# The end of a transformer block rearranged into strands on their own PSUM banks, with 1/sqrt on GpSimd

## The chip, the cores and the metric

The kernel runs on one core of a Trainium2 chip. The metric is the device time of one execution in microseconds (us); less is better. Times of several executions are given as a median with their range. The profile is of one further execution.

## What is computed

One block with adaptive layer norm: attention with 32 heads of 16 columns over 2048 tokens of width 512, then a gated feed-forward network (FFN) of width 1792. Inputs and output are bf16. `B_x` is not used.

```python
def _layernorm(x, axis=-1, eps=1e-05):
    return (x - mean(x)) / sqrt(var(x) + eps)
def _A_ref(x, wqkv, wo):              # H = 32, Dh = 16
    q, k, v = heads(x @ wqkv)
    p = softmax(q @ k.T * Dh ** -0.5)
    return merge(p @ v) @ wo
def _B_ref(x, w_gate, w_up, w_down):
    return (gelu(x @ w_gate) * (x @ w_up)) @ w_down
sa, ca, ga, sb, cb, gb = split(silu(c) @ w_mod, 6)
h = _layernorm(x) * (1 + ca) + sa
x = x + ga * _A_ref(h, A_wqkv, A_wo)
h = _layernorm(x) * (1 + cb) + sb
x = x + gb * _B_ref(h, B_w_gate, B_w_up, B_w_down)
```

## The kernel before

The names of engines: PE does matmuls, ACT (ScalarE) activations, DVE (VectorE) and POOL (GpSimd) elementwise work, SP issues DMAs.

**Recorder and planner.** The whole program is written by a planner in Python that runs when the kernel is built. `rec` notes each instruction with what it reads and writes and works out the semaphore waits; `model` and `cost` keep an estimate of the time at which each engine is free. Each engine then executes its own list in order, and waits only where a semaphore says so. Side work is kept as generators (`side_wo`, `side_ffn`, `near_end` and others) and as tasks, lists of steps for one engine after another, which `step` places when the estimate says that their inputs are there. Matmuls of zero value to the result, here called fillers, are put in when the estimate (`short`, `FILL`) shows PE less busy than wanted.

**Attention.** The 2048 query tokens are cut into seven sets, `SETS`, of 512, 512, 256, 256, 256, 128 and 128. Within a set the heads go in eight groups of four (`qd`), spread over the four 32-row strips of PE. Score matmuls write to `ps_sc`, six banks of PSUM used as two halves of three; one ACT instruction does the exponential of up to three banks (1536 columns) into `E`, and now and then one bank is given to DVE instead, which does an exponential in seven steps (`exp_vec`). A gate on `credit` and the backlog decides when. The PV matmuls add into `ps_pv`; V has a column of ones, so that one output row of 17 is the softmax's denominator. `pv_round` copies the finished group to `osb`, takes the denominator out through DRAM (`scr_den`, `den`, reciprocal into `rden`, `scr_rec`) and spreads it over partitions into `rb` with four DMAs; then `onorm` = `osb` x `rb`. The last groups (`qd` 6 and 7) of the last two sets do without DRAM: a matmul with the selector `self32` spreads the denominator in PSUM, and DVE takes the reciprocal of it (`near_end`).

**Behind each set.** `side_wo` multiplies `onorm` with `wo` in bank `ps_mi` and adds to x in `xs`; then come statistics (`ln_stat`: bn_stats, bn_aggr), 1/sqrt(var + eps) in eight small DVE instructions (`ln_rstd_step`: a bit-trick guess and two Newton steps), the normalise (`ln_norm`), transposes, modulation, and the FFN (`side_ffn`), also through `ps_mi`, with gelu made of tanh. All this runs beside the attention of the next sets, in the one bank `ps_mi`.

**The end** (`tail`). Call the last two token tiles A (set 5) and B (set 6). `side_ffn` does the first two chunks (`EARLY`) of A's FFN in `ps_mi`. When A's part is done and all attention with all PV matmuls has been written, `tail` loads ACT's gelu table and interleaves two generators: `tail_end` for B (denominators of group 7 in a bank of `ps_sc`, `wo` into `ps_sc` bank 4 over an identity matmul of x, statistics, normalise, transposes, modulation, then `tail_ffn` on six banks) and `tail_ffn` for the rest of A on banks 0 to 3, with A's down projection in `ps_pv` and B's in `ps_mi`. The denominator of B's group 6 is a side work item behind A's part, in `ps_mi`. An ACT copy puts B's attention output from PSUM to `xs`, and the statistics of B follow that copy; modulation of B is shared, half on ACT and half on DVE.

Of the kernel before, what the change touches and what calls it, by code (L numbers as in the profile page):

```python
# [5 lines left out]
ACT = mybir.ActivationFunctionType  # L6
# [41 lines left out]
EARLY = 2  # L48
BACK = 10
# [28 lines left out]
class _Recorder:  # L78
# [165 lines left out]
    def model(self, op, t, cost):  # L244
# [38 lines left out]
    def cost(self, eng, out, ins, kind):  # L283
# [8 lines left out]
        if eng == "pool":  # L292
            return n * 3.0 + 100
# [117 lines left out]
class _Kernel(_Recorder):  # L411
# [12 lines left out]
    def alloc(self):  # L424
# [41 lines left out]
        self.nwx = sb("nwx", [P, NT], FP32)  # L466
# [4 lines left out]
        self.nb = sb("nb", [P, NT], FP32)  # L471
# [16 lines left out]
    def prologue(self):  # L488
# [24 lines left out]
        self.affine_select(self.ident[:, :], [[-1, P]], ALU.not_equal, 1.0, 0, 1)  # L513
        self.memset(pool, self.rm4[:, :], 1.0)
# [4 lines left out]
        self.memset(pool, self.vaug[:, :, :].rearrange("p t (h c) -> p t h c", c=VW)[:, :, :, DH:VW], 1.0)  # L519
# [13 lines left out]
        self.ln_rstd(0, 4)  # L533
        self.mod_cols(self.scp[:, 1, 0:8], 0)
# [35 lines left out]
    RSTD = 8  # L570

    def ln_rstd_step(self, a, b, i):

        x, y, t = self.nwx[:, a:b], self.rstd[:, a:b], self.nwt[:, a:b]
        if i == 0:
            self.ts("dve", x, self.mv[:, a:b, 1], EPS, -0.5, ALU.add, ALU.mult)
        elif i == 1:
            self.ts("dve", y.bitcast(I32), x.bitcast(I32), -0.5, 1597463007.0 - 2.0 ** 30 - 2.0 ** 22, ALU.mult, ALU.add)
        elif i % 3 == 2:
            self.tt("dve", t, y, y, ALU.mult)  # L580
        elif i % 3 == 0:
            self.tt("dve", t, t, x, ALU.mult)
        else:
            self.stt(y, t, 1.5, y, ALU.add, ALU.mult)

    def ln_rstd(self, a, b):
        for i in range(self.RSTD):
            self.ln_rstd_step(a, b, i)
# [3 lines left out]

    def ln_nb(self, a, b):
        self.stt(self.nb[:, a:b], self.mv[:, a:b, 0], -1.0, self.rstd[:, a:b], ALU.mult, ALU.mult)

    def ln_norm_pool(self, t, dst):
        self.ts("pool", dst, self.xs[:, t, :], self.rstd[:, t:t + 1], self.nb[:, t:t + 1], ALU.mult, ALU.add)
# [124 lines left out]
    def side_first(self):  # L722
# [4 lines left out]
        def norms(t0):  # L727
            g = t0 // 4
            self.task([lambda i=i: self.ln_rstd_step(t0, t0 + 4, i) for i in range(self.RSTD)]
                      + [lambda t=t: self.ln_norm(t0 + t, self.tb1[:, g % 2, t, :]) for t in range(4)], ("ln", g),  # L730
                      self.after([("st", t) for t in range(max(8, t0), t0 + 4)]))
# [256 lines left out]
    def background(self, t):  # L988
        while self.free["dve"] <= t + 150 and self.step("dve", max(self.free["dve"], t) + 40):
            pass  # L990

    def force(self):
        if not self.step("dve", None):
            assert self.step("act", None)

    def plan(self, ends, nsplit):
# [25 lines left out]
        w.append((lambda: self.near_end(k + 1, 6, self.mi[:, 0:P]), s0, s0))  # L1022
# [48 lines left out]
    def stream(self):  # L1071
# [37 lines left out]
        filler = self.ident[:, :], self.km[0][:, 0, 0:512]  # L1109
# [26 lines left out]
        while rp < len(rounds):  # L1136
# [19 lines left out]
            if tq is not None and tq <= t + 30:  # L1156
# [78 lines left out]
        self.tail(len(SETS) - 2, len(SETS) - 1)  # L1235
# [57 lines left out]
    def pv_round(self, rnd, acc):  # L1293
# [5 lines left out]
        if r != NKT // kpb - 1:  # L1299
            return  # L1300
# [4 lines left out]
        if sets[0] >= len(SETS) - 2 and len(sets) == 1 and qd >= 6:  # L1305
# [34 lines left out]
    def tail(self, ka, kb):  # L1340

        self.require([("part", ka)])
        self.act(self.tcol[:, 0:1], self.tcol[:, 0:1], ACT.Gelu_apprx_tanh)
        gens = [self.tail_end(kb), self.tail_ffn(ka, self.pv[:, :], range(0, 4), 0)]
        nxt = [None] * len(gens)
        while True:
            t = self.pe_now()
            while self.step("act", max(self.free["act"], t) + 40) or self.step("dve", max(self.free["dve"], t) + 40):
                pass
# [23 lines left out]
            if best is None:  # L1373
                if all(g is None for g in gens) and not self.tasks and not self.work:
                    break
                continue
            f, nxt[best[1]] = nxt[best[1]], None
            f()

    def tail_end(self, k):  # L1380
# [3 lines left out]
        bank = self.scp[:, 4, :]  # L1384
        for x in self.near_end(k, 7, self.scp[:, 5, 0:W]):
            if x is not END:
                yield x and x[1]
# [5 lines left out]
        self.task([lambda: self.ln_stat(tile, bank)] + self.ln2_steps(k, bank), ("ln2", k))  # L1393
        self.task([("act", lambda: self.act(self.xs[:, tile, :], bank, ACT.Copy))], ("x1", k))
        yield from self.until(("ln2", k))
        for h in range(2):
            pb = self.scp[:, 4 + h, :]
# [7 lines left out]
    def tail_ffn(self, k, down, banks, e0):  # L1405
# [3 lines left out]
        nb = [0]  # L1409

        def up(ci, w):
            if nb[0] == 2 and k == len(SETS) - 1:
                yield from self.until(("p", k - 1, len(chunks) - 1))
            bk = self.scp[:, banks[nb[0] % len(banks)], :]
# [5 lines left out]
        first = EARLY if k < len(SETS) - 1 else 0  # L1420
# [3 lines left out]
        for ci in range(first, len(chunks) + 1):  # L1424
            if ci < len(chunks):
# [4 lines left out]
                          ("g", k, ci))  # L1430
# [54 lines left out]
```

## Time and profile before

| | us |
|---|---|
| median of 3 runs | 908.53 |
| range of these | 906.87 to 908.95 |
| the profiled execution | 911.24 |
| its span in the trace | 909.4 |
| busy in the span: ACT | 877.2 (96%) |
| DVE | 833.9 (92%) |
| PE | 826.3 (91%) |
| POOL | 3.6 |

All times in the trace are in us from the start of the span, and lengths of single instructions in us or, where it says mean, in ns. PE's busy time counts overlapping matmuls once; PEld is its weight load. The span is the part that the trace covers; the rest of an execution's time lies around it. A group's row gives line, engine, operation, output and input names and shapes, the count, then busy time and mean length of one in ns, then the idle time ahead of them and what ended it. PEclk is the granted clock of PE as a share of full speed.

### The profile page before, as it was taken

How to read it: one execution, taken by the hardware profiler on the slowest of the kernel's cores; microseconds unless marked ns; L12 is line 12 of the kernel's file. 1: busy time of each engine (PE TensorE's matmuls, PEld its weight loads, DVE VectorE, ACT ScalarE, POOL GpSimd, SP SyncE). 2: the span in 40 equal slices, each digit the busy share in tenths (PEclk: the TensorE clock that was granted, in tenths of full speed). 3: DMA queues.
4: the chain of work that ended last, by engine and by line, in shares of the span. 5: the costliest groups of instructions: out<-in, count | busy, mean ns of one | idle time of the engine just before them, and what ended most of it. 6: DMA issues, size and time to landing. Idle time of an engine off the chain costs nothing.

```text
span 909.4 us, 20886 instructions
## 1 busy us (share of the span) xinstructions
PE 826.3 (91%) x8708; PEld 292.0 (32%) x8708; DVE 833.9 (92%) x2114; ACT 877.2 (96%) x754; POOL 3.6 (0%) x11
## 2 busy tenths in 40 slices
PE   8899998988899899998999999999999988989988
PEld 3333322222222222222233222333443334334455
DVE  7779999999998999999998999998999889989874
ACT  5999999999999999999999999999999999999992
POOL 1000000000000000000000000000000000000000
PEclk9999999999999999999999999999999999999999
DMA  9001320000100000000000000000000000000000
GB/s 300 2 25 41 118 86 13 13 15 13 54 13 14 1 13 14 13 14 25 20 14 14 14 9 13 16 25 20 15 8 20 19 9 14 20 15 14 18 11 13
DMA packets 35337, 25.19 MB, mean 28 GB/s; under 512 B 19053, under 2 KB 31082, under 8 KB 35242
## 3 DMA queue, kind: packets, MB, share of 16 engines
q1 hardware_dynamic: 32858, 22.28, 8.7%
q10 hardware_dynamic: 2384, 1.57, 0.6%
q8 instruction: 68, 1.11, 0.5%
q14 instruction: 27, 0.22, 0.1%
HBM read 21.23 MB, written 2.61 MB: 26 GB/s over the span
## 4 chain that ended last, share of the span: by engine, by line
ACT 83%; PE 6%; DVE 5%; DMA 4%; SPq 1%; issue 0%; DVEq 0%
ACT E L319 81%; PE ps_sc L306 3%; ACT wreg L319 2%; PE ps_mi L306 2%; DMA rb<-scr_rec 1%; DMA scr_rec<-rden 1%; SPq L369 1%; DMA mreg<-in_w_mod_dram 1%; PE ps_pv L306 1%; DMA den<-scr_den 0%; DVE qT L323 0%; DVE qT L336 0%; DVE dx L331 0%; DVE wreg L323 0%; DVE wreg L340 0%
## 5 line engine op out<-in xcount | busy, mean ns | idle before, releaser
L319 ACT ACTIVATE E<-ps_sc 128x1536 bf16<-128x1536 f32 (+2 forms) x698 | 849.9, 1440 | 10.6 <-PE ps_sc L306 10.1
L306 PE MATMUL ps_pv<-E,vaug 128*17 128x256 bf16 (+2 forms) x2912 | 182.4, 300 | 1.8 <-DVE vaug L340 0.8
L306 PE MATMUL ps_sc<-qT,kme 32*128 32x256 bf16 (+2 forms) x1600 | 169.0, 304 | 12.9 <-ACT E L319 8.0
L306 PE MATMUL ps_sc<-qT,kmo 32*128 32x256 bf16 (+2 forms) x1664 | 169.1, 298 | 11.4 <-ACT E L319 7.8
L306 PE MATMUL ps_sc<-kme,ident 128*128 128x512 bf16 x334 | 106.7, 384 | 35.5 <-ACT E L319 32.0
L331 DVE TENSOR_SCALAR dt<-ps_sc 128x512 int32<-128x512 f32 x189 | 129.6, 687 | 5.7 <-PE ps_sc L306 3.0
L306 PE MATMUL ps_mi<-wreg,mreg 128*128 128x256 bf16 (+2 forms) x624 | 118.4, 308 | 6.8 <-DVE wreg L340 3.9
L306 PEld LDWEIGHTS ps_sc<-qT,kme 32*128 32x128 bf16 x1600 | 48.7, 92 | 127.0 <-ACT E L319 70.4
L306 PEld LDWEIGHTS ps_sc<-qT,kmo 32*128 32x128 bf16 x1664 | 49.8, 92 | 121.4 <-ACT E L319 70.8
L306 PEld LDWEIGHTS ps_pv<-E,vaug 128*17 128x17 bf16 x2912 | 53.7, 88 | 100.5 <-issue 88.5
L331 DVE TENSOR_SCALAR dx<-dt 128x512 f16<-128x512 uint16 x189 | 78.2, 420 | 0.1
L323 DVE TENSOR_TENSOR qT<-qT,dx 128x512 f16<-128x512 f16 x188 | 77.0, 419 | 0.7
L306 PEld LDWEIGHTS ps_mi<-wreg,mreg 128*128 128x128 bf16 x624 | 49.6, 97 | 55.0 <-issue 21.4
L336 DVE SCALAR_TENSOR_TENSOR qT<-dt,qT 128x512 int16<-128x512 int32 x94 | 64.4, 686 | 0.4
L306 PE MATMUL ps_mi<-dreg,hreg 128*128 128x512 bf16 x210 | 62.7, 384 | 0.8 <-DVE wreg L336 0.3
L323 DVE TENSOR_TENSOR ed<-ed,dx 128x512 f16<-128x512 f16 x128 | 53.1, 419 | 0.5
L306 PEld LDWEIGHTS ps_sc<-kme,ident 128*128 128x128 bf16 x334 | 22.6, 97 | 90.4 <-ACT E L319 87.7
L336 DVE SCALAR_TENSOR_TENSOR ed<-dt,ed 128x512 int16<-128x512 int32 x64 | 43.9, 686 | 0.2
L340 DVE CAST wreg<-ps_mi 128x512 bf16<-128x512 f32 x51 | 35.1, 688 | 8.1 <-PE ps_mi L306 7.5
L306 PE MATMUL ps_mi<-hreg,wreg 128*128 128x512 bf16 x120 | 39.4, 386 | 0.7 <-DVE qT L331 0.2
L323 DVE TENSOR_TENSOR wreg<-wreg 128x512 bf16<-128x512 bf16 (+1 forms) x74 | 38.6, 521 | 0.2
L306 PE MATMUL ps_mi<-wo,onorm 128*128 128x512 bf16 x120 | 35.3, 384 | 1.4 <-DVE xw L323 1.3
(135 smaller groups left out, 770.7 us busy)
## 6 DMA issues: line engine op xcount, KB each, us to landing
rb<-scr_rec SPq DMA_DIRECT2D x64, 64.0 KB, 2.0
rb<-scr_rec SPq DMA_DIRECT2D x116, 32.0 KB, 1.8
mreg<-in_w_mod_dram SPq DMA_DIRECT2D x1, 2048.0 KB, 14.3
out_dram<-xs SPq DMA_DIRECT2D x16, 128.0 KB, 1.7
mreg<-in_B_w_gate_dram SPq DMA_DIRECT2D x4, 448.0 KB, 5.2
mreg<-in_B_w_up_dram SPq DMA_DIRECT2D x4, 448.0 KB, 5.0
dreg<-in_B_w_down_dram SPq DMA_DIRECT2D x3, 512.0 KB, 4.9
wreg<-in_A_wqkv_dram SPq DMA_DIRECT2D x3, 384.0 KB, 10.6
```

The lines of the kernel that those rows point to most:

```text
L306: return self.rec("pe", lambda e: e.matmul(out, lhsT, rhs, start=start, stop=stop, tile_position=tp), [lhsT, rhs], [out], cost=(n, int(rhs ...
L319: return self.rec("act", lambda e: e.activation(out, in_, func, scale=scale, **kw), rd, wr, cost=self.cost("act", out, [in_], "act"))
L323: return self.rec(eng, lambda e: e.tensor_tensor(out, a, b, op), [a, b], [out], cost=self.cost(eng, out, [a, b], "tt"))
L331: return self.rec(eng, lambda e: e.tensor_scalar(out, a, s1, s2, **kw), rd, [out], cost=self.cost(eng, out, [a], "ts" if len(rd) == 1 else ...
L336: return self.rec("dve", lambda e: e.scalar_tensor_tensor(out, a, s, b, op0=op0, op1=op1), rd, [out], cost=self.cost("dve", out, [a, b], " ...
L340: return self.rec(eng, lambda e: e.tensor_copy(out, in_), [in_], [out], cost=self.cost(eng, out, [in_], "ts"))
L369: return e.dma_start(out, in_)
```

## The change

The diff does the following.

- **1/sqrt.** `ln_rstd_step` and its eight DVE steps go. `ln_rstd` is two POOL instructions: add eps, then raise to the power -0.5 held in `half`. The tasks that used the steps now hold one POOL step, and `background`, `force` and `tail` also serve tasks of POOL. The cost estimates for POOL are changed. The memset of the ones in `vaug` moves behind the first such pair on POOL.
- **Statistics ahead of the copy.** In `tail_end` the statistics of B come first, and the ACT copy of the bank, as well as the 1/sqrt and the normalise, wait for them. All four modulations of B are on ACT.
- **Strands and banks.** The main loop ends when the last score matmul has been written (`pos < nseq`), no longer with the last PV; the remaining PV rounds become a generator `rest` of `tail`. The denominators of B's groups 6 and 7 are generators of their own (`tail_den`), each with its own bank. The six banks of `ps_sc` are split in two lists of three: `f` for B (denominators, `wo`, transposes, then its FFN), `l` for the rest of A.
- **Order.** B's steps are put at the head of the task list; A's `tail_ffn` waits for its part by a key in place of `tail` waiting at once. The gelu table is loaded once A's second tanh is written. `tail` may write fillers.
- **The late gate.** An exponential goes to DVE only while `credit` is under 1600, in place of 2600, from the end of the fifth set on.

```diff
+NEAR = 6
...
-            op.t1 = t + cost + (107 if eng == "act" else 92)
+            op.t1 = t + cost + {"act": 107, "dve": 92, "pool": 120}[eng]
...
-            return n * 3.0 + 100
+            return n * (30.0 if n <= 4 else 3.0) + 200
...
+        self.memset(pool, self.half[:, :], -0.5)
...
     def ln_rstd(self, a, b):
-        for i in range(self.RSTD):
-            self.ln_rstd_step(a, b, i)
+        r = self.rstd[:, a:b]
+        self.ts("pool", r, self.mv[:, a:b, 1], EPS, None, ALU.add)
+        self.tt("pool", r, r, self.half[:, 0:b - a], ALU.pow)
...
-        return ([lambda i=i: self.ln_rstd_step(a, b, i) for i in range(self.RSTD)]
+        return ([("pool", lambda: self.ln_rstd(a, b))]
...
-        w.append((lambda: self.near_end(k + 1, 6, self.mi[:, 0:P]), s0, s0))
...
-        while rp < len(rounds):
+        while pos < nseq:
...
-                        and len(mem) == CH and slack > -100 and self.credit < 2600):
+                        and len(mem) == CH and slack > -100 and self.credit < (2600 if pos < ends[-3] else 1600)):
...
-        self.tail(len(SETS) - 2, len(SETS) - 1)
+
+        def rest():
+            for k in range(rp, len(rounds)):
+                while True:
+                    for a in list(active):
+                        if a[0] in self.have:
+                            self.slot[a[1]] = a[2]
+                            active.remove(a)
+                    if pv_ready(k) is not None:
+                        break
+                    yield None
+                yield lambda k=k: self.pv_mms(rounds[k], acc_of(rounds[k]))
+                self.pv_done(rounds[k], acc_of(rounds[k]))
+        self.tail(len(SETS) - 2, len(SETS) - 1, c % 2, rest())
...
-    def tail(self, ka, kb):
-
-        self.require([("part", ka)])
-        self.act(self.tcol[:, 0:1], self.tcol[:, 0:1], ACT.Gelu_apprx_tanh)
-        gens = [self.tail_end(kb), self.tail_ffn(ka, self.pv[:, :], range(0, 4), 0)]
+    def tail(self, ka, kb, half, rest):
+        f = [self.scp[:, CH * half + i, :] for i in range(CH)]
+        l = [self.scp[:, CH * (1 - half) + i, :] for i in range(CH)]
+        gens = [rest] + [self.tail_den(kb, qd, f[qd - 5]) for qd in range(NEAR, 8)]
+        gens += [self.tail_end(kb, f, l), self.tail_ffn(ka, self.pv[:, :], l, 0, ("part", ka))]
...
+            if not table and ("gelu", ka, EARLY - 1) in self.have:
+                self.act(self.tcol[:, 0:1], self.tcol[:, 0:1], ACT.Gelu_apprx_tanh)
...
+    def tail_den(self, k, qd, bank):
+        q0, W = SETS[k]
+        _, lo, hi = self.osb_span(((k,), qd, q0, W))
+        osb, rb = self.osb[:, lo:hi], self.rb[:, lo:hi]
+        yield from self.until(("osb", k, qd))
+        yield lambda: self.mm(bank[:, 0:W], self.self32[:, :], osb)
+        self.task([lambda: self.recip(rb, bank[:, 0:W]),
+                   lambda: self.tt("dve", self.onorm[:, qd, OCOL[k]:OCOL[k] + W], osb, rb, ALU.mult)],
+                  ("onorm", k, qd), first=True)
...
-        self.task([lambda: self.ln_stat(tile, bank)] + self.ln2_steps(k, bank), ("ln2", k))
-        self.task([("act", lambda: self.act(self.xs[:, tile, :], bank, ACT.Copy))], ("x1", k))
+        self.task([lambda: self.ln_stat(tile, bank)], ("s2e", k), first=True)
+        self.task([("act", lambda: self.act(self.xs[:, tile, :], bank, ACT.Copy))], ("x1", k), self.after([("s2e", k)]))
+        self.task(self.ln2_steps(k, bank), ("ln2", k), self.after([("s2e", k)]), first=True)
...
-                self.modulate("act" if i == 0 else "dve", self.t2T[:, dc, c0:c0 + W],
+                self.modulate("act", self.t2T[:, dc, c0:c0 + W],
...
-        yield from self.tail_ffn(k, self.mi[:, :], (4, 5, 0, 1, 2, 3), 4)
+        yield from self.tail_ffn(k, self.mi[:, :], f, 4, None)
...
-            if nb[0] == 2 and k == len(SETS) - 1:
-                yield from self.until(("p", k - 1, len(chunks) - 1))
```

More of the change, by code (lines that the diff above doesn't have):

```diff
@@ L533, in prologue @@
         self.ln_rstd(0, 4)
+        self.memset(pool, self.vaug[:, :, :].rearrange("p t (h c) -> p t h c", c=VW)[:, :, :, DH:VW], 1.0)
         self.mod_cols(self.scp[:, 1, 0:8], 0)
@@ L988, in background @@
     def background(self, t):
+        while self.step("pool", max(self.free["pool"], t) + 40):
+            pass
         while self.free["dve"] <= t + 150 and self.step("dve", max(self.free["dve"], t) + 40):
@@ L1108, in stream @@
         virt = 0.0
-        filler = self.ident[:, :], self.km[0][:, 0, 0:512]
+        self.filler = filler = self.ident[:, :], self.km[0][:, 0, 0:512]
         def take(n):
@@ L1298, in pv_round, with pv_done @@
         self.pv_mms(rnd, acc)
-        if r != NKT // kpb - 1:
+        self.pv_done(rnd, acc)
+    def pv_done(self, rnd, acc):
+        u, r, g0 = rnd
+        sets, qd, q0, W = u
+        if r != NKT * W // 512 - 1:
             return
@@ L1383, in tail_end @@
         c0, tile = BCOL[k], q0 // P
[L1384 to L1387, printed above, removed]
+        bank = f[0]
         yield from self.until("wo")
@@ L1419, in up @@
             return bk
-        first = EARLY if k < len(SETS) - 1 else 0
+        if key is not None:
+            yield from self.until(key)
+        first = 0 if lead else EARLY
         for ci in range(first):
```

49 lines of the change are left out of this document (19 added, 30 removed).

## The prediction, on record before the result was known

> **What bounds the kernel now.** I read the page's busy shares first, then the stretches, then the groups by form, then the timeline of the last 30 us. Of the page, these lines:
>
> ```profile
> span 909.4 us, 20886 instructions
> PE 826.3 (91%) x8708; PEld 292.0 (32%) x8708; DVE 833.9 (92%) x2114; ACT 877.2 (96%) x754; POOL 3.6 (0%) x11
> ACT 83%; PE 6%; DVE 5%; DMA 4%; SPq 1%; issue 0%; DVEq 0%
> ```
>
> All of PE, DVE and ACT are over 90% busy, but the chain that ended last lies on ACT for 83% of the span. The stretches tell why, and where this ends (us, then busy time of PE, PEld, DVE, ACT, POOL, then PEclk, DMA share, GB/s):
>
> ```profile
> 300.00:860.00 560.00, 514.46 (x5861) 180.03 (x5859) 531.08 (x1353) 558.61 (x473) 0.00 (x0) 1.00 0.06 15
> 882.16:885.58 3.42, 1.67 (x33) 1.39 (x34) 2.16 (x6) 2.29 (x4) 0.00 (x0) 1.00 0.05 14
> 885.58:888.99 3.41, 3.41 (x11) 1.52 (x11) 2.25 (x5) 0.00 (x0) 0.00 (x0) 0.50 0.00 0
> ```
>
> Up to the end of attention ACT idles 1.4 us in 560: there only fewer ACT columns count. After it ACT is nearly idle, PE is half idle for 3.42 us and then runs 3.41 us at half clock. The kernel is thus a body paced by ACT and an end paced by a chain. The end is what the diff rewrites.
>
> **The body.** Groups by form of ACT and DVE, and one slot of ACT in the chain:
>
> ```profile
> L319 ACT ACTIVATE E<-ps_sc 128x1536 bf16<-128x1536 f32 x475 | 690.2, 1580 | 2.3 <-PE ps_sc L306 1.9
> L319 ACT ACTIVATE E<-ps_sc 128x1024 bf16<-128x1024 f32 x217 | 245.9, 1160 | 0.1
> L336 DVE SCALAR_TENSOR_TENSOR rstd<-nwt,rstd 128x4 f32<-128x4 f32 x12 | 1.9, 161 | 0.3
> 815.06 0.51 ACT wreg L319
> ```
>
> The order of the changed kernel's instructions has 474 exponentials of 1536 columns and 218 of 1024, so 512 columns leave ACT: 1580 - 1160 = 420 ns, **-0.42 us**. One more exponential runs on DVE (190 for 189). Eleven groups of eight small DVE instructions go, 88 x 0.16 = 14 us of DVE's 833.9. I give them nothing but that one exponential, since ACT paces the body; DVE has no more than those 14 us to turn into gain. In their place stand 22 GpSimd instructions. From the first of such a group to the normalise behind it, and two rows of POOL:
>
> ```profile
> 871.79 0.15 DVE L331 TENSOR_SCALAR nwx<-mv 128x1 f32<-128x1 f32 x1
> 873.33 0.41 DVE L331 TENSOR_SCALAR hreg<-xs,mv,rstd 128x512 bf16<-128x512 bf16 x1
> 2.03 2.27 POOL L347 MEMSET vaug<- 128x512 bf16 x1
> 1.65 0.45 POOL L350 TENSOR_SCALAR_AFFINE_SELECT rm<-rm 128x4 f32<-128x4 f32 x2
> ```
>
> A group costs DVE 873.33 - 871.79 = 1.54. No power on POOL is in this trace. Nearest rows: 4 columns take 0.45/2 = 0.22 each, 512 columns 2.27. A pair, with its two handovers, thus costs between 0.5 and 2.3 or more. I take **0.7**, by the 4-column row it resembles, 0.22 plus some 0.12 for each wait. In the body the DVE's normalise waits behind it, with all that is queued after: 0.7 for 1.54, no loss. The memset of vaug moves behind the first pair and ahead of the next, whose statistics are not ready before the first exponential, so it is free. The tighter late gate only decides which exponentials DVE takes; the counts above hold its result. Fillers go from 422 to 414 on a PE that is not the bound: nothing.
>
> **The end before.** Engine by engine in order of time (start, length, instruction, idle before it):
>
> ```profile
> 880.93 1.53 ACT L319 ACTIVATE E<-ps_sc 128x1536 bf16<-128x1536 f32 x1
> 882.26 0.70 ACT L319 ACTIVATE wreg<-wreg 128x512 bf16<-128x512 bf16 x1
> 882.51 0.40 PE L306 MATMUL ps_pv<-E,vaug 128*17 128x128 bf16 x15 [0.43 <-ACT E L319]
> 882.96 0.29 DVE L340 COPY osb<-ps_pv 128x128 f32<-128x128 f32 x1
> 884.37 0.29 DVE L323 TENSOR_TENSOR onorm<-osb,rb 128x128 bf16<-128x128 f32 x1 [1.12 <-DMA rb<-scr_rec]
> 885.31 0.57 PE L306 MATMUL ps_mi<-osb,self 128*128 128x128 f32 x2 [1.40 <-DVE wreg L336]
> 886.95 2.48 PE L306 MATMUL ps_sc<-wo,onorm 128*128 128x512 bf16 x6
> 889.91 0.59 PE L306 MATMUL ps_sc<-wo,onorm 128*128 128x512 bf16 x2
> 891.25 0.70 DVE L359 BATCH_NORM_STATS2 st<-ps_sc 128x6 f32<-128x512 f32 x1 [3.22 <-ACT xs L319]
> 894.22 0.81 DVE L331 TENSOR_SCALAR dx<-ps_sc,mv,rstd 128x512 bf16<-128x512 f32 x1
> 895.09 0.40 PE L310 MATMUL ps_sc<-ident,dx 128*128 128x128 bf16 x4
> 896.38 3.93 PE L306 MATMUL ps_sc<-wreg,mreg 128*128 128x128 bf16 x64 [0.35 <-DVE wreg L331]
> 906.04 0.69 DVE L323 TENSOR_TENSOR xw<-ps_mi,gb 128x512 bf16<-128x512 f32 x1 [0.83 <-PE ps_mi L306]
> 906.77 0.42 DVE L323 TENSOR_TENSOR xs<-xs,xw 128x512 bf16<-128x512 bf16 x1
> ```
>
> Let e be the end of the last exponential's slot on ACT, 882.26 here, where the next instruction starts. From e to the end are 909.4 - 882.26 = **27.1 us**, in four pieces: e to the statistics 8.99, statistics to transposes 3.84, transposes to the last evacuation (xw) 10.95, evacuation and output 3.36. In the first piece DVE waits 1.12 us for a transfer, PE 1.40 us behind it for bank ps_mi, and six 512-column matmuls take 2.48, 0.41 each, at half clock.
>
> **The end after, step by step.** By the order of the changed program the last tanh stands ahead of the last exponential, so e moves by +0.51 - 0.42 = **+0.09**. What follows needs more prices, from the timeline and the chain, and the late transfer:
>
> ```profile
> 864.83 0.49 PE L306 MATMUL ps_mi<-osb,self 128*128 128x128 f32 x2
> 865.36 0.96 DVE L343 RECIPROCAL rb<-ps_mi 128x128 f32<-128x128 f32 x1 [0.39 <-PE ps_mi L306]
> 866.35 0.29 DVE L323 TENSOR_TENSOR onorm<-osb,rb 128x128 bf16<-128x128 f32 x1
> 900.14 1.03 PE L306 MATMUL ps_mi<-dreg,hreg 128*128 128x512 bf16 x4
> 895.41 0.81 ACT L319 ACTIVATE wreg<-ps_sc,modB 128x128 bf16<-128x128 bf16 x2 [1.39 <-PE ps_sc L310]
> 896.73 3.58 PE ps_sc L306 x61
> 891.21 2.84 PE L306 MATMUL ps_sc<-wreg,mreg 128*128 128x128 bf16 x48
> 882.45 1.79 DMA rb<-scr_rec
> 857.41 1.72 SPq L369 DMA_DIRECT2D rb<-scr_rec  x4
> 879.43 3.44 SPq L369 DMA_DIRECT2D rb<-scr_rec  x4
> ```
>
> The last four issues of rb took SP 3.44 where the earlier four took 1.72, and landed at 884.24, e + 1.98. SP's list is in the same order in both kernels, so I let the long issue recur. But the chain starts earlier: between the end of the first 16 gate matmuls, which stand next to its reciprocal, and the last exponential lie four sets of twelve score matmuls now, two before, so two exponential slots, 2 x 1.33 = 2.7 us. It lands at e - 0.7. Then DVE in its new order, times after e (starts spaced by the lengths above less about 0.06 of overlap): onorm of group 5 at -0.7, the product of chunk 0 -0.4, of chunk 1 0.0 (0.63), reciprocal of group 6 +0.6 (0.90), product +1.5 (0.36), copy of group 7 +1.8 (PE had its PV done at +0.7). PE self32 +2.15, reciprocal +2.7 (0.53 later, as 864.83 to 865.36), onorm +3.7, wo +4.0. Ahead of that wo stand seven down matmuls, 0.22 each, behind the wo of group 6 at +2.4: PE is free at 4.1. Statistics at **+4.5** (before 8.99).
>
> No ACT copy comes first now: 891.25 - 890.5 = 0.7 of the saving. Then bn_stats and bn_aggr 0.95, POOL 0.7, dx 0.87: transposes could start at +7.0. PE itself has one down and 48 gate/up matmuls to do (2.84 in the trace; the next matmul starts 2.77 after the first) and is ready at **+7.3**, so a POOL pair up to 1.0 is covered and above that each us counts. Modulation is now four on ACT, spaced 0.34, where DVE took two: the last is ready 0.32 + 3 x 0.34 + 0.47 = 1.81 after the transposes; before, the up matmuls ran freely 1.64 after them (896.73). So 0.2 dearer, and 10.95 becomes 11.1: xw at **+18.5**. At the end the other tile's last four down matmuls and its two DVE steps now stand behind this tile's: 1.17 + 1.17, then 2.18 for the output (907.22 to 909.4): **+23.0**. Three banks for six cost nothing: the gate of the next chunk is read long before its bank returns.
>
> Sum: 23.0 - 27.1 + 0.1 = **-4.0**. The profiled execution took 911.24, span 909.4; it would become 907.2. It lies 2.7 above the median of the runs, 908.53, which range over 2.1. Taking off the same 4.0 gives **904.5**; what the two do not share is a rival below.
>
> **Half clock, row and rule.** PEclk is 0.50 exactly from 885.58 to 888.99, after a stretch with PE busy 1.67 of 3.42. In the new order PE has from e + 0.3 on PV, eight wo, two self32 and eight down before the ups, with one idle piece near e + 1.5 of under 1 us, so I expect 1.00. The Trainium skill, TensorE: Matmul & The Clock Gate, Part 1, says that such a window is free-running and does not start with the kernel, so an ordinary run of before could escape the half clock; this trace shows one phase only. By that rule the sum would be up to 1.7 less.
>
> **Rivals.**
> (a) *Ordinary runs of before lack the half clock and the long SP issue.* Half of 3.41 is 1.7 us that the profiled run lost and others may not. Then -4.0 becomes -2.3: **906.2**. For it: the profiled run's 2.7 above the median. Against: the PE gap comes from the order of instructions. Chance 0.15.
> (b) *Body drift.* A new schedule shifts 690 exponentials against PE and DVE. If ACT's idle time, 2.3 + 0.1 = 2.4 by the two rows of exponentials, more than doubles, by 2.8 say: **907.3**, 0.09. If it vanishes: **902.1**, 0.09. This contains that the change does not do what it says to DVE.
> (c) *Slower: the POOL pair is long.* Place: the ten normalise steps in the body, where DVE's queue stands behind POOL, and the last one on the chain. With a pair of p the loss is 10 (p - 1.54) + (p - 1.0) if ACT feels all of it. It eats 4.0 and 1.8 more (0.2%, about what a measurement of this kernel can tell) at p = 2.0; at p = 2.27, the vaug row, it is 8.6: **913**. Against: 512 columns there, 1 to 4 here. Chance 0.08.
> (d) *The first power pays a start-up.* It stands ahead of the first normalise:
>
> ```profile
> 9.03 1.38 DVE L331 TENSOR_SCALAR dreg<-xs,mv,rstd 128x512 bf16<-128x512 bf16 x4
> 10.92 1.12 PE L310 MATMUL ps_sc<-ident,dreg 128*128 128x128 bf16 x16
> ```
>
> The normalise ends at 10.41 and PE reads it at 10.92, 0.5 later. The pair has 1.54 + 0.5 = 2.0; with 0.7 and a start-up as long as the 2.27 row it is 0.9 late: **905.4**. Chance 0.04. GPSIMD Engine Reference, Instruction dispatch, in the Trainium skill has the first call of a freshly loaded library at about 6 us, by which the time would be about 909; no run here shows it.
>
> **How the numbers follow.** The forecast has 0.55, its own range 902.8 to 906.3. Faster: 0.53 of it, 0.12 of (a), 0.09 of (b), 0.02 of (d), together 0.76. Same (906.7 to 910.3): 0.02 of the forecast, 0.03 of (a), 0.08 of (b), 0.02 of (d): 0.15. Slower: (c) and 0.01 of (b), 0.09. The range leaves out (c), part of the quick (b) and little else: **902.3 to 908.0**.
>
> **What would show it.** Right: PEclk 1.00 throughout the last 30 us; one tanh ahead of the last exponential; statistics within 5 us of e, straight after the last wo; the POOL pair under 1 us with the 48 gate/up matmuls ending after it; the other tile's xw and xs as DVE's last two instructions. Wrong: ACT idle over 5 us in the body, DVE waiting on POOL for over 1.5 us at a time, e later than 883, or the end more than 24 us after e.

## The result, and the profile after

The changed kernel takes **911.96 us** (median of 5 runs, 910.51 to 913.33), the kernel before, measured beside it, 908.53 (906.52 to 909.78): a ratio of **1.0041**, 95% interval 1.0021 to 1.0061. 904.5 was forecast, with 0.09 for slower. The profiled execution took 912.22; its page:

```profile
span 910.5 us, 20673 instructions
PE 793.2 (87%) x8566; PEld 290.2 (32%) x8700; DVE 828.2 (91%) x2031; ACT 877.9 (96%) x756; POOL 17.5 (2%) x34
ACT 73%; DVE 11%; PE 8%; DMA 5%; SPq 1%; issue 1%; POOL 1%; DVEq 0%
```

The chain that ended last lies on ACT for 73% where it was 83%, and DVE's share went from 5 to 11%: something keeps ACT waiting. The stretches say where. Before (us, then busy time of PE, PEld, DVE, ACT, POOL):

```profile
20.00:880.00 860.00, 786.85 (x8312) 269.01 (x8308) 803.45 (x2026) 857.81 (x724) 0.31 (x1) 1.00 0.08 22
...
600.00:750.00 150.00, 137.76 (x1755) 53.81 (x1750) 137.92 (x371) 149.47 (x128) 0.00 (x0) 1.00 0.06 16
750.00:880.00 130.00, 120.02 (x1893) 54.37 (x1890) 116.08 (x313) 129.14 (x110) 0.00 (x0) 1.00 0.07 16
```

and after:

```profile
20.00:880.00 860.00, 752.10 (x8055) 264.43 (x8185) 798.28 (x1963) 853.61 (x721) 10.73 (x17) 1.00 0.08 22
...
600.00:750.00 150.00, 131.58 (x1717) 53.71 (x1739) 140.08 (x367) 148.47 (x128) 2.81 (x4) 1.00 0.07 16
750.00:880.00 130.00, 112.61 (x1757) 51.17 (x1777) 110.01 (x281) 126.58 (x108) 1.74 (x4) 0.99 0.07 15
```

ACT's idle time from 20 to 880 us is 860 - 857.81 = 2.19 before and 860 - 853.61 = **6.39** after; 2.6 of the 4.2 more lie behind 750 us. (PE's busy time is not to be compared: some of its records are missing after.) The exponentials of the changed kernel, by forms:

```profile
L320 ACT ACTIVATE E<-ps_sc 128x1536 bf16<-128x1536 f32 x474 | 685.9, 1555 | 5.4 <-PE ps_sc L307 4.8
L320 ACT ACTIVATE E<-ps_sc 128x1024 bf16<-128x1024 f32 x218 | 243.2, 1135 | 1.6 <-PE ps_sc L307 1.5
```

The end, in its timeline:

```profile
886.17 1.54 ACT L320 ACTIVATE E<-ps_sc 128x1536 bf16<-128x1536 f32 x1
886.60 0.29 DVE L324 TENSOR_TENSOR onorm<-osb,rb 128x128 bf16<-128x128 f32 x1 [1.17 <-DMA rb<-scr_rec]
...
887.73 1.28 ACT L320 ACT_TABLE_LOAD   x1
...
891.69 0.70 DVE L360 BATCH_NORM_STATS2 st<-ps_sc 128x6 f32<-128x512 f32 x1 [0.66 <-PE ps_sc L307]
892.43 0.18 DVE L363 BATCH_NORM_AGGREGATE mv<-st 128x2 f32<-128x6 f32 x1
...
893.01 0.58 POOL L324 TENSOR_TENSOR rstd<-rstd,half 128x1 f32<-128x1 f32 x1
893.72 0.81 DVE L332 TENSOR_SCALAR dx<-ps_sc,mv,rstd 128x512 bf16<-128x512 f32 x1 [1.11 <-POOL rstd L324]
...
894.59 0.40 PE L311 MATMUL ps_sc<-ident,dx 128*128 128x128 bf16 x4
894.92 1.50 ACT L320 ACTIVATE wreg<-ps_sc,modB 128x128 bf16<-128x128 bf16 x4 [0.39 <-PE ps_sc L311]
...
905.79 0.69 DVE L324 TENSOR_TENSOR xw<-ps_mi,gb 128x512 bf16<-128x512 f32 x1 [0.83 <-PE ps_mi L307]
...
907.77 0.43 DVE L324 TENSOR_TENSOR xs<-xs,xw 128x512 bf16<-128x512 bf16 x1
```

The last exponential starts at 886.17; with its slot of 1.33, e is 887.50 (before 882.26). Statistics stand at e + 4.2, the transposes at + 7.1, B's xw at + 18.3, the end at **+ 23.0**, before + 27.2 (the span is 909.42 there, so the prediction's 27.1 is 27.2). So the end gained 4.2, and e came 5.2 later: 4.2 of it the idle time above, 0.5 more work of ACT between the first exponential and e (863.88 us for 863.40), and 0.6 in the prologue:

```profile
8.70 2.28 POOL L348 MEMSET vaug<- 128x512 bf16 x1
8.78 3.30 DVE L332 TENSOR_SCALAR dreg<-xs,mv,rstd 128x512 bf16<-128x512 bf16 x4 [1.49 <-POOL rstd L324]
...
17.23 3.71 ACT L320 ACTIVATE E<-ps_sc 128x1536 bf16<-128x1536 f32 x3 [0.58 <-PE ps_sc L307]
```

The first four normalises take 3.30 where they took 1.38, with the moved memset now beside them, and the first exponential starts at 17.23 (16.66 before). The Trainium skill, SBUF — State Buffer, Who interferes with whom, has a DVE instruction in a two-port mode share a port pair with GpSimd, which the first to issue holds for its whole instruction; the trace agrees as far as it shows: one normalise lasts 2340 ns, about as long as the memset beside it, and the others go back to 0.4 us. (That this normalise is in such a mode isn't to be seen in it.)

**Where ACT waits.** The largest single stall of the body, 1.30 us, rows in the order of time:

```profile
864.40 2.97 SPq L370 DMA_DIRECT2D rb<-scr_rec  x4
...
868.97 0.29 DVE L324 TENSOR_TENSOR onorm<-osb,rb 128x128 bf16<-128x128 f32 x1 [2.09 <-DMA rb<-scr_rec]
869.18 0.95 DVE L344 RECIPROCAL rb<-ps_mi 128x128 f32<-128x128 f32 x1
...
870.41 1.03 PE L307 MATMUL ps_mi<-wo,onorm 128*128 128x512 bf16 x4 [1.74 <-DVE rb L344]
...
871.82 2.79 ACT L320 ACTIVATE E<-ps_sc 128x1536 bf16<-128x1536 f32 x2 [1.30 <-PE ps_sc L307]
```

SP issues the four transfers of rb in 2.97 (1.72 otherwise), and DVE's product waits 2.09 for them. The reciprocal, which reads bank `ps_mi`, stands right behind that product on DVE. PE waits for the reciprocal in front of a `wo` matmul into that bank, and the score matmuls behind it come late for ACT. Near 788 us a late product (behind an issue of 1.72) reaches PE by another way: PE waits 0.63 and 0.54 for two DVE instructions behind it, and right after that runs at half clock:

```profile
785.93 0.43 DVE L324 TENSOR_TENSOR onorm<-osb,rb 128x256 bf16<-128x256 f32 x1 [1.72 <-DMA rb<-scr_rec]
...
788.09 0.39 PE L307 MATMUL ps_sc<-qT,kmo 32*128 32x256 bf16 x4 [0.63 <-DVE dt L332]
789.02 0.28 PE L307 MATMUL ps_pv<-E,vaug 128*17 128x256 bf16 x3 [0.54 <-DVE osb L341]
...
786.18:789.59 3.41, 1.86 (x30) 0.65 (x30) 3.41 (x10) 3.36 (x4) 0.00 (x0) 1.00 0.00 0
789.59:793.00 3.41, 3.41 (x24) 0.65 (x24) 3.17 (x9) 1.57 (x3) 0.00 (x0) 0.50 0.16 43
```

PE is busy 1.86 of 3.41 and then runs 3.41 us at 0.50; ACT works 1.57 of those. And POOL, by forms and by waits:

```profile
L324 POOL TENSOR_TENSOR rstd<-rstd,half 128x4 f32<-128x4 f32 x6 | 6.4, 1068 | 0.5
L324 POOL TENSOR_TENSOR rstd<-rstd,half 128x1 f32<-128x1 f32 x2 | 1.2, 578 | 0.2
...
DVE onorm L324 <- DMA rb<-scr_rec: 11.0, 14, 2.1
DVE hreg L332 <- POOL rstd L324: 4.1, 5, 1.1
DVE dreg L332 <- POOL rstd L324: 3.0, 2, 1.5
DVE dx L332 <- POOL rstd L324: 1.1, 1, 1.1
```

A power of four columns takes 1068 ns, one of one column 578; DVE waits 4.1 + 3.0 + 1.1 = 8.2 us for POOL in all, and not at all before. The waits for rb aren't new; the kernel before has

```profile
DVE onorm L323 <- DMA rb<-scr_rec: 8.8, 14, 1.2
```

and six issues of four rb transfers that took SP over 2.2 us, where the changed kernel has two. So a late rb alone doesn't make ACT wait.

### The profile page after: what moved, and what is told of

Its sections match the earlier page's. It is cut to its first block, busy times and chain, and to the rows that moved or that the text cites. A ratio compares the mean times of both kernels' runs of the same rounds, so it can differ in the third digit from the quotient of the medians.

```text
span 910.5 us, 20673 instructions
## 1 busy us (share of the span) xinstructions
PE 793.2 (87%) x8566; PEld 290.2 (32%) x8700; DVE 828.2 (91%) x2031; ACT 877.9 (96%) x756; POOL 17.5 (2%) x34
## 3 DMA queue, kind: packets, MB, share of 16 engines
q10 hardware_dynamic: 2384, 1.57, 0.6%
q8 instruction: 68, 1.11, 0.5%
## 4 chain that ended last, share of the span: by engine, by line
ACT 73%; DVE 11%; PE 8%; DMA 5%; SPq 1%; issue 1%; POOL 1%; DVEq 0%
ACT E L320 70%; PE ps_sc L307 4%; PE ps_mi L307 3%; ACT wreg L320 2%; DMA rb<-scr_rec 2%; DMA scr_rec<-rden 2%; SPq L370 1%; PE ps_pv L307 1%; DVE dt L332 1%; DVE qT L324 1%; DVE qT L337 1%; DVE dx L332 1%; DMA den<-scr_den 1%; DVE osb L341 1%; DVE onorm L324 1%
## 5 line engine op out<-in xcount | busy, mean ns | idle before, releaser
L307 PE MATMUL ps_sc<-qT,kmo 32*128 32x256 bf16 (+2 forms) x1664 | 164.9, 299 | 22.4 <-ACT E L320 17.0
L307 PE MATMUL ps_sc<-qT,kme 32*128 32x256 bf16 (+2 forms) x1600 | 166.6, 304 | 19.0 <-ACT E L320 12.8
L307 PE MATMUL ps_sc<-kme,ident 128*128 128x512 bf16 x289 | 94.0, 384 | 41.2 <-ACT E L320 37.7
L307 PE MATMUL ps_mi<-wreg,mreg 128*128 128x256 bf16 (+2 forms) x603 | 112.6, 305 | 10.3 <-DVE wreg L341 4.6
L324 DVE TENSOR_TENSOR qT<-qT,dx 128x512 f16<-128x512 f16 x190 | 79.2, 421 | 1.1
L307 PE MATMUL ps_mi<-dreg,hreg 128*128 128x512 bf16 x184 | 56.7, 384 | 2.7 <-issue 1.7
L307 PE MATMUL ps_mi<-wo,onorm 128*128 128x512 bf16 x107 | 33.1, 391 | 3.4 <-DVE rb L344 1.7
L307 PE MATMUL ps_mi<-hreg,wreg 128*128 128x512 bf16 x106 | 34.1, 385 | 2.3 <-issue 0.8
```

Source lines behind the costliest of these rows:

```text
L307: return self.rec("pe", lambda e: e.matmul(out, lhsT, rhs, start=start, stop=stop, tile_position=tp), [lhsT, rhs], [out], cost=(n, int(rhs ...
L324: return self.rec(eng, lambda e: e.tensor_tensor(out, a, b, op), [a, b], [out], cost=self.cost(eng, out, [a, b], "tt"))
```

## Experiments

Three explanations of the loss in the body were set against each other. **P**: the length of the GpSimd pair, which DVE waits out. **D**: every edit makes the planner lay out another order, and orders differ by luck. **O**: the planner holds a price for the pair (two operations of 320 ns by its estimate, at four columns) that is too short, and lays out worse orders for it. The price called measured below is two operations of 940 ns; the pair's two take 337 and 1068 on average, so it lies above the trace; no run has a price of just that length. All ratios are to the kernel before on the same chip. "Idle" is ACT's from 20 to 880 us of the profiled execution, "end" the time from e to the end of the span.

| | ratio, 95% interval | idle | end |
|---|---|---|---|
| before | 1 | 2.19 | 27.2 |
| changed kernel | 1.0041 (1.0021, 1.0061) | 6.39 | 23.0 |
| e1 strands alone | 0.9968 (0.9952, 0.9984) | 2.04 | 24.4 |
| e2 1/sqrt alone | 1.0041 (1.0026, 1.0057) | 5.34 | 27.2 |
| e3 before, other order | 1.0012 (0.9999, 1.0025) | 3.97 | 26.9 |
| e4 no power | 1.0040 (1.0025, 1.0055) | 9.23 | 23.2 |
| e5 strands, B on GpSimd | 0.9982 (0.9964, 0.9999) | 2.73 | 24.6 |
| e6 gate 2600 | 1.0026 (1.0006, 1.0045) | 5.83 | 26.4 |
| e7 measured price | 0.9974 (0.9955, 0.9993) | 4.11 | 22.5 |
| e8 changed, other order | 1.0005 (0.9987, 1.0024) | 4.61 | 22.9 |
| e9 memset back | 1.0048 (1.0030, 1.0067) | 8.93 | 23.3 |
| e10 changed, other order | 1.0017 (1.0003, 1.0031) | 6.40 | 23.2 |
| e11 measured price, other order | 0.9984 (0.9971, 0.9996) | 2.94 | 23.3 |
| e12 measured price, memset back | 0.9970 (0.9958, 0.9981) | 2.46 | 22.4 |
| e13 = e2, measured price | 1.0043 (1.0027, 1.0059) | 2.39 | 32.3 |
| e14 = e1, gate 1600 | 0.9984 (0.9967, 1.0000) | 2.75 | 22.9 |
| e15 = e12, gate 2600 | 1.0003 (0.9986, 1.0019) | 2.68 | 27.5 |
| e16 = e12, other order | 0.9967 (0.9952, 0.9981) | 3.95 | 23.3 |
| e17 = e12, other order | 0.9977 (0.9963, 0.9990) | 1.92 | 22.3 |
| e18 = e12, other order | 1.0007 (0.9994, 1.0020) | 1.79 | 27.0 |

**e1, e2: the parts apart.** e1 is the changed kernel with DVE's 1/sqrt everywhere, the estimates, the memset and the gate of before; e2 is the kernel before with the 1/sqrt on GpSimd and its estimates.

> The end of the changed kernel (strands, banks, statistics ahead of the copy, modulation on ACT) behind the 1/sqrt on DVE, the estimates and the gate of before, so that the first 11636 of 11952 recorded instructions are those of before. e is the end of the last exponential's slot on ACT; it was 882.26 before and 887.50 after. If the end is worth what the forecast gave it and the loss lies in the body: e at 882.3 to 883, from e to the end of the span 23.0 plus 0.3 to 0.6 for the eight DVE steps, so 906 to 906.5 for the span, 3 us less than before. If the strands themselves cost the 5 us (the PV matmuls and denominators out of the main loop hold up the last exponentials): e at 886 or later and the time at or above that of before.

> The 1/sqrt on GpSimd alone, with its estimates and the moved memset, in the kernel before, with the end of before. Theory P (the pair on GpSimd, 1.3 to 1.9 us where 0.7 was forecast, holds up DVE's queue in the body): DVE waits about 8 us on GpSimd as in the changed kernel, e at 885 to 888, time 3 to 5 us above before. Theory D (any change of an estimate makes the planner draw another schedule, whose stalls of ACT differ by some us): the same DVE waits, but e anywhere between 880 and 888, and its stalls at other places than those of the changed kernel.

The strands alone gain 0.32% and leave the body as it was, idle 2.04. The 1/sqrt alone costs 0.41%, all of it ahead of e: its end is that of before to 0.1. The loss comes with the 1/sqrt. But e is 884.5, just short of P's 885, and ACT stalls near 652 and 790 us as in the changed kernel, where D expected other places.

**e3: another order of the kernel before.** One estimate of the planner is changed by 10 ns.

```diff
-op.t1 = self.dma_free + 1000
+op.t1 = self.dma_free + 1010
```

> The kernel before with one number of the planner's estimate changed: a DMA is taken to land 10 ns later. No work is added or taken away. Theory P and every theory by which the parts of the change cost time: within 0.5 us of before. Theory D: e moves by 2 to 5 us from 882.26, most likely later, since before is then one draw of many and a favourable one.

The same work in another order: 0.12% slower, idle 3.97. An order alone moves the idle time by 1.8 us, not by 4.2 here. The 2 to 5 us by which D expected e to move don't show: it is 881.9 for 882.3.

**e4: the pair short, the order kept.** A product stands in place of the power, so 1/sqrt isn't computed.

```diff
-self.tt("pool", r, r, self.half[:, 0:b - a], ALU.pow)
+self.tt("pool", r, r, self.half[:, 0:b - a], ALU.mult)
```

> The changed kernel with all instructions at the same places, but the GpSimd power replaced by a multiplication with the same operands, so that 1/sqrt is not computed (its output isn't the reference's). The order of all engines stays. Theory P: the pair falls from 1.3 to 1.9 us to about 0.5 to 0.6, DVE's 8.2 us of waiting on GpSimd nearly go, and e falls from 887.5 by 3 to 5. Theory D: e falls by 0.5 to 1 only (the pair in the prologue), and ACT's stalls near 788 and 869 stay.

Groups, waits and the stretch from 20 to 880 us of e4:

```profile
L324 POOL TENSOR_TENSOR rstd<-rstd,half 128x4 f32<-128x4 f32 x6 | 1.4, 227 | 0.5
...
DVE onorm L324 <- DMA rb<-scr_rec: 15.1, 16, 3.1
DVE hreg L332 <- POOL rstd L324: 1.3, 2, 0.7
DVE dreg L332 <- POOL rstd L324: 1.3, 2, 0.6
...
20.00:880.00 860.00, 780.20 (x8149) 263.55 (x8146) 794.73 (x1952) 850.77 (x718) 5.42 (x17) 0.99 0.08 22
```

The operation falls from 1068 to 227 ns, DVE's waits for POOL to 1.3 + 1.3 + 0.7 (B's) = 3.3, and the time stays, idle even 9.23, e even 889.4. **P falls**: DVE does wait for POOL, but that isn't what ACT waits for. The waits for rb remain. D, which kept both stalls, has one of them: 3.59 us near 869, but under 0.2 at a time near 790.

**e5: e1 with the GpSimd pair for B alone.**

> The strands alone as in e1, and the GpSimd pair for the 1/sqrt of tile B only, which stands behind all exponentials; the list of instructions up to the end is that of before. In e1 the stretch from e to the end took 24.36. B's pair takes 0.23 + 0.58 by the trace of the changed kernel, in place of eight DVE steps of 1.5. If the end is a chain that this shortens: from e to the end 23.0 to 23.8, e within 0.5 of e1's 881.96, and 0.5 to 1.2 us less than e1, 3 to 4.5 us under before. If transposes wait for the gate and up matmuls of A anyway: the same as e1.

End 24.6, as e1's 24.4, and the forecast of 23.0 to 23.8 is missed: the pair gives the end nothing. In e1 the eight small instructions take 1.55 (888.02 to 889.57); in e5 DVE waits 1.45 for the same step.

**e6: the late gate back to 2600 in the changed kernel.**

```diff
-self.credit < (2600 if pos < ends[-3] else 1600)
+self.credit < 2600
```

> The changed kernel with the late gate of before (credit under 2600 to the end). Its order is that of the changed kernel up to the late sets and that of e2 there. Theory G (the tighter gate moves work so that the last denominators come late: the 1.56 us of ACT near 869): that stall goes, e falls from 887.5 to about 884.5 as in e2, and the time by some 2.5 to 3. Theory D: e anywhere within 884 to 888; the 2 us near 789 stay in either case, since the order there is the same.

The stall near 869 goes, as theory G said (0.32 is left), and those near 790 stay, but others come, idle changes little (5.83), and the end is 3.4 longer. The gate isn't what makes ACT idle, and it is part of the gain at the end. What it does to the length of the body is read with e14 and e15.

**e7, e8: the price raised; another order with the short one.** e7 gives the planner the measured price, e8 the short one and the 10 ns of e3.

```diff
-return n * (30.0 if n <= 4 else 3.0) + 200
+return n * (160.0 if n <= 4 else 3.0) + 300
```

> The changed kernel with the planner's price of GpSimd raised to what the trace shows (a pair of 4 columns some 2 us with its handovers, 0.9 before), nothing else. If the loss is a plan that does not know how long the pair is: DVE's waits on GpSimd fall from 8.2 to under 4, e falls to 883 to 884, time within 1 us of before. Theory D: another draw, with stalls at other places, e between 883 and 889 without regard to the waits on GpSimd.

> The changed kernel with the planner taking a DMA to land 10 ns later; same work. Theory D: e moves by 1 to 4 us either way, and the stalls near 789 and 869 go or move. If the loss belongs to the parts of the change wherever they stand: e stays within 1 us of 887.5.

The price makes the same kernel 0.67% faster (0.9974 for 1.0041); 10 ns elsewhere make it 0.36% faster. In e7 DVE's waits for POOL fall to 3.7, as forecast, but e is 885.8, not 883 to 884. In e8 both stalls go, as D said, yet e is 886.6, within the 1 us of 887.5 that spoke for the parts. Both O and D are alive.

**e9: the memset of vaug at its old place**, all else in the changed kernel's order.

> The changed kernel with the memset of vaug at its old place, ahead of the first GpSimd pair; every other instruction stands in the same order on every engine as in the changed kernel. If the moved memset costs something: the first four normalises go back from a mean of 526 ns to about 410, the first exponential starts about 0.5 earlier, and the time is 0.3 to 0.6 us (0.03 to 0.07%) less, ratio to the kernel before about 1.0035. If it costs nothing: as the changed kernel, 1.004. If the loss in the body is one of the order of instructions, the stalls of ACT near 789 us and 869 us stay where they are; if it is the noise of one execution, they go elsewhere.

The first four normalises of e9:

```profile
8.87 1.38 DVE L332 TENSOR_SCALAR dreg<-xs,mv,rstd 128x512 bf16<-128x512 bf16 x4 [1.49 <-POOL rstd L324]
```

1.38 again, and the first exponential starts at 15.21. The forecast of a shorter time is missed all the same: 1.0048. ACT stalls at the same two places, behind the same `wo` for 3.80 us at once in place of 1.30, after a rb issue of 3.84. e4, in the changed kernel's order too, has only the second (3.59). So the weak places belong to the order; whether and how long ACT stalls there, to the execution.

**e10 to e12: orders under both prices.** e10 raises ACT's estimate by 5 ns (107 to 112) under the short price; e11 is e7 with the 10 ns, e12 is e7 with the memset back.

> The changed kernel with 5 ns more in the planner's estimate of an ACT instruction's latency, 112 for 107: the same work, laid out in another order. Theory D (the order is one draw among several, and a draw moves the time by 0.1 to 0.4%): a ratio to the kernel before anywhere in 0.998 to 1.005, and not that of the changed kernel to within 0.1%. Theory O (GpSimd planned too short makes every such plan bad in the body): 1.002 to 1.006, with DVE's waits on POOL at 8 us again and over 11 us of overruns of ACT slots.

> The kernel with the measured GpSimd price in the planner, drawn again by 10 ns in the estimate of a transfer. Theory O (the price that the planner holds for the pair decides): DVE's waits on POOL 3 to 5 us again, ratio 0.996 to 0.999, as with the true price alone (0.9974). Theory D (draws alone): anywhere in 0.997 to 1.003.

> The measured GpSimd price in the planner and the memset of vaug at its old place: a candidate that beats both kernels. By the true price 0.9974, less 0.5 us of prologue: 0.9968, with an interval of some 0.0015 around it. Theory D (draws alone): anywhere in 0.996 to 1.002, since the order in the body is another again.

Waits and stretch of e12:

```profile
DVE onorm L324 <- DMA rb<-scr_rec: 4.0, 7, 1.0
DVE hreg L332 <- POOL rstd L324: 2.2, 2, 1.2
...
20.00:880.00 860.00, 758.46 (x8214) 269.03 (x8341) 797.50 (x1963) 857.54 (x725) 9.71 (x17) 1.00 0.08 22
```

The power takes 1080 ns there as before, but DVE's waits for rb are 4.0 for 11.0 (8.8 before), and ACT idles 2.46. e10 has 6.40 of idle, as O says, though its 1.0017 lies just below O's range. e12 beats both kernels.

**e13 to e16: price, gate or luck.** e13 is e2 with the measured price, e14 is e1 with the gate of 1600, e15 is e12 with that of 2600, e16 is e12 with the 10 ns.

> The kernel before with the 1/sqrt on GpSimd alone, as in the second experiment (1.0041), but with the measured GpSimd price in the planner. Price theory: the loss goes, ratio 0.999 to 1.0015, and from the first exponential to the end of the last 865.5 to 866.5 us in place of 867.0. Gate theory: the gate is 2600 in both, so the 1.0041 stays, 1.003 to 1.005. Draw: anywhere between.

> The strands with DVE's 1/sqrt everywhere (0.9968) and the late gate of 1600. Gate theory: the body is 2 us or more longer, 867 to 868 from the first exponential to the end of the last, and the ratio 0.999 or above. Price theory: the gate costs nothing in a body without the pair, 864.5 to 866 and 0.995 to 0.998.

> The fastest kernel so far (measured price, memset back, 0.9970) with the gate of 2600. Gate theory: the body gets shorter, by up to 2 us, and so does the time, 0.995. Price theory: the body stays within 1 us of 866.4; if the end is 3 us longer again, as in the sixth experiment, where the gate of 2600 came with an end of 26.4 us, the ratio is 1.000.

> The fastest kernel drawn again by 10 ns in the estimate of a transfer. Price theory: 0.996 to 0.9985, a fourth plan with the measured price that beats the kernel before. Draw: 0.996 to 1.003, and if it is over 1.000 the claim that the price decides falls.

e13 splits what its expectation had in one: the body is healed (idle 2.39 for 5.34, from the first exponential to e 864.4 us), but the end is 32.3, and the ratio stays at 1.0043: both tanh of A come behind e, and PE runs at half clock from 887 to 894. e15 shows the same place. ACT in e15, then DVE's last row but one:

```profile
874.74 5.50 ACT L320 ACTIVATE E<-ps_sc 128x1536 bf16<-128x1536 f32 x4
882.45 0.63 ACT L320 ACTIVATE wreg<-wreg 128x512 bf16<-128x512 bf16 x1 [2.21 <-DVE wreg L324]
884.20 0.63 ACT L320 ACTIVATE wreg<-wreg 128x512 bf16<-128x512 bf16 x1 [1.12 <-DVE wreg L324]
...
904.12 0.69 DVE L324 TENSOR_TENSOR xw<-ps_pv,gb 128x512 bf16<-128x512 f32 x1 [1.23 <-PE ps_pv L307]
```

and in e12:

```profile
879.80 0.82 ACT L320 ACTIVATE wreg<-wreg 128x512 bf16<-128x512 bf16 x1
880.32 1.65 ACT L320 ACTIVATE E<-ps_sc 128x1536 bf16<-128x1536 f32 x1
```

In e15 both tanh of A come behind the last exponential and wait 2.21 and 1.12 for DVE, which still has A's side work; A is then last, at 904.12. In e12 the last tanh stands ahead of the last exponential. With the gate of 2600 DVE has taken more exponentials (191 for 189) and carries its side work past e. The gate of 1600 is worth 0.33% to e12 and nothing to the strands with DVE's 1/sqrt (e14 against e1: intervals overlap). From the first exponential to e, in e12 and then in e15:

```profile
15.22:881.65 866.43, 763.84 (x8277) 272.37 (x8408) 801.90 (x1972) 863.16 (x729) 10.99 (x19) 1.00 0.09 24
15.20:880.03 864.83, 764.21 (x8253) 271.57 (x8378) 802.91 (x1978) 861.34 (x727) 10.99 (x19) 1.00 0.09 24
```

So the gate theory is half right: the gate of 1600 makes the body 1.6 us longer here, 1.8 in e14 (867.0, in that theory's range) against e1, 2.1 in the changed kernel against e6. But in e12 this is work that ACT does ahead of e (863.16 for 861.34), and e14 and e15 idle no more than 2.75 and 2.68. It is not the loss by idle time.

**e17, e18: two more orders under the measured price**, ACT's estimate up by 5 ns (as e10) and DVE's by 5 (92 to 97).

> The kernel with the measured GpSimd price and the memset back, drawn again by 5 ns in the estimate of an ACT instruction's latency, as the tenth experiment did with the short price (1.0017, ACT idle 6.4 us between 20 and 880 us). Price theory: ACT idle under 4.3 there, ratio 0.996 to 0.999. Draw theory: idle anywhere from 2 to 9 us, ratio 0.996 to 1.004; over 4.6 us the separation of the two prices is gone.

> The same drawn by 5 ns in the estimate of a DVE instruction's latency, 97 for 92: the order changes on nearly every line. Price theory: ACT idle under 4.3 us between 20 and 880 us, ratio 0.996 to 0.999. Draw theory: idle anywhere from 2 to 9 us, ratio 0.996 to 1.004.

Idle 1.92 and 1.79, as O says; the same 5 ns on ACT gave 6.40 under the short price. The ratio of e18 misses it: its second tanh of A waits 3.94 behind e, and the end is 27.0, with the gate of 1600. That gate alone doesn't keep DVE's backlog out of the end.

**What is shown, what is open.** With the gate of 1600 every order under the measured price idles 1.8 to 4.1 us (four plans: e7 and e12, which differ in the memset's place alone, e11 and e16 likewise, e17, e18), every one under the short price 4.6 to 8.9 (three: the changed order with e9, e8, e10). With the gate of 2600 it is 5.34 and 5.83 (e2, e6) against 2.39 and 2.68 (e13, e15). Four pairs differ in the price alone, and each idles less under the measured one: 6.39 and 4.11 (changed kernel, e7), 4.61 and 2.94 (e8, e11), 8.93 and 2.46 (e9, e12), 5.34 and 2.39 (e2, e13).

Each of these is one execution, and the window matters: counted from the first exponential to e, e16 (measured price) idles 4.76 and e8 (short) 4.61. The median times can be read without it. If a run's end is taken off its ratio (of some 909 us), then by this estimate the part ahead of e is 4.8 to 8.3 us longer than before under the short price and 0.8 to 2.8 under the measured one, both with the gate of 1600; e14, which has no pair, has 2.8. With the gate of 2600 it is 3.2 and 3.7 (e6, e2), against 0.0 and -1.2 (e15, e13), and -0.1 in e1 without the pair. So the price decides about the body: with the measured one the pair costs it no more than DVE's eight steps.

What in the orders does it isn't shown. The short price plans the normalise earlier behind the pair, but e4, where the chip comes closer to that plan, is no better. Late rb transfers reach ACT through DVE's queue at the two places above, but their sum doesn't tell the orders apart (8.8 us before, with idle 2.19; 6.7 in e2, with 5.34). The granted clock tells more: between 20 us and e, PE ran at half clock for 3.4 us or more in the profiles of the changed kernel, e2, e4, e6, e9 and e10, not in e8; under the measured price only in e7 and e16, which idle most in their group; and in neither before nor e1. Part of the idle time is thus ACT waiting for a PE at half clock (3.41 - 1.57 = 1.84 us near 790 in the changed kernel); what in the order leaves PE idle ahead of it stays open.

## Why the prediction was wrong, point by point

- **The failed step**: "In the body the DVE's normalise waits behind it, with all that is queued after: 0.7 for 1.54, no loss", and with it a body of -0.42. It costs the body by counting instructions and keeps the idle time of before. The counts came true (474 exponentials of 1536, 218 of 1024), yet idle went from 2.19 to 6.39, and e, forecast at +0.09, came at +5.24: 4.19 idle, 0.57 in the prologue, 0.48 more work. It isn't DVE's wait that costs this (e4). A new price in the planner is a new order of the whole program, and those laid out under the short price leave ACT idle more (four pairs of runs).
- **The pair's price**, 0.7, was mis-sized: DVE's wait for it is 1.49 at four columns and 1.11 at one, inside the bounds of 0.5 to 2.3. By rival (c)'s formula 1.49 is no loss, and e4 agrees.
- **Rival (b)**, ACT's idle time more than doubled, was the right mechanism. By its two rows it went from 2.4 to 7.0, 4.6 more for the 2.8 priced, and it had 0.09.
- **The memset, "free"**: wrong. The next statistics weren't the ones to look at; the four normalises right beside it took 3.30 for 1.38. The first exponential came 0.57 later than before (2.0 later than in e9, which also lacks a stretch of half clock there); the times don't resolve it.
- **The late gate, "the counts above hold its result"**: wrong in kind. It makes the body 1.6 to 2.1 us longer and the end shorter, so part of the end's gain is its own: strands 2.8 (e1), gate 1.4 more (e14).
- **The end** was right: 23.0 as forecast, statistics + 4.2 (4.5), transposes + 7.1 (7.3), xw + 18.3 (18.5), one tanh ahead of the last exponential, A's xs last. The pair was just covered, PE's 48 ups ending as dx did. PEclk was 1.00 from 880.5 to 908.0. One hit is luck: the long SP issue didn't recur at the last burst (1.71, done at 883.64), but the product waited for its transfers until 886.60, 2.96 behind the issue, where before it was 1.50. So it came at e - 0.9 for the forecast - 0.7 by two errors that cancel.
- **Rivals (a) and (d)**: e1 gains in ordinary runs what its profile gains (0.9968 is 2.9 us, its profile 3.1), which speaks against (a), though the interval goes down to 1.5. The first power took 1.05, as the second: the start-up of about 6 us that the Trainium skill, GPSIMD Engine Reference, Instruction dispatch, gives for the first call of a freshly loaded kernel doesn't show.
- Of "Wrong if", e past 883 and idle over 5 us came true: the signs were right, their chance too small.

## What to carry to other kernels

Where a planner lays out the program, a new operation changes the order of everything, so measure its price on the chip before it goes into the estimates: here a price somewhat above its measured length turned 1.0041 into 0.9974, with nothing else changed. A local gain of 4 us in 900 is of the size that a new order gives or takes by itself (1.0005 to 1.0048 under one price), so try each part alone and with several orders, and read ACT's idle time in the body apart from the end. A gate that gives work to another engine has to be read at the end too, where that engine's backlog comes due.

## What the runs showed of the hardware

- A power on GpSimd: 1068 ns for 128x4, 578 for 128x1, where a product took 227 for 128x4.
- Four DMA issues of SP took 1.7 us as a rule, and 2.2 to 3.84 now and then: six of 47 times before, two in the changed kernel, eight in e12. At one place of an order they took 2.97 and 3.84 (e9), and the product behind them waited 2.09 and 3.51.
- PE, busy 1.86 of 3.41 us, ran at half clock for the next 3.41 (changed kernel, from 789.59 on), as it did before after 1.67 of 3.42: a stall of PE can be paid twice.
